# Row pitch of a resident matmul operand: 642 elements widened to 656

## The chip, the cores and the metric

The kernel runs on one core of a Trainium2 chip. The metric is the device time of one execution in microseconds (us). A "step" below is the time from the start of one matmul to the start of the next, read from the trace record by record, in nanoseconds (ns). Step lists and sums of steps are worked out from those records. They stand in ordinary fences, and lines copied from the profile in fences marked as such.

## The reference, cut to what matters

Input x is 2048 x 640, bf16. The result is `g * a + (1 - g) * b`, with a gate g, a linear attention a, and an MLP mixer b.

```python
qkv = (x @ wqkv)...                       # 32 heads of 20
pq, pk = phi(q), phi(k)
kv = einsum("bhsd,bhse->bhde", pk, v)     # the sum over s
z  = pk.sum(over s)
a  = (pq @ kv) / (pq @ z + 1e-6) @ wo
b  = x1 + gelu(layernorm(x1) @ w3) @ w4,  x1 = x + shifted(gelu(layernorm(x) @ w1)) @ w2
```

Since v = x @ wv, the sum over s can be taken first: `pk.T @ v = (pk.T @ x) @ wv`. The kernel does that. Its "g units" compute `pk.T @ x`, with a column of ones beside x that gives z for one more column in every second matmul (in the changed kernel the steps of 321 columns are 136.5 ns in the mean, those of 320 columns 136.0). A stretch of the kernel that does one such job is called a stage. The matmuls of the g units have x as their *moving operand* (`rhs` in the code), and `pk` as their weights (`lhsT`).

## The kernel before

x stays in SBUF for the whole kernel, as 16 chunks of 128 rows. Each partition holds one row of each chunk, one after the other. D is 640, and two elements follow each row: the first is the one for z.

```python
x_sb = const.tile([P, NCH, D + 2], BF16)           # P = 128, NCH = 16
...
nc.gpsimd.memset(x_sb[:, :, D:D + 1], 1.0)
...
def g_unit(j):                                      # five of them, HD = 320
    pt = pair()                                     # [P, 2, 512] f32 in PSUM; each half is called a bank
    for c in range(NCH):
        w = pk[:, c, :].rearrange("p (m j) -> p j m", j=DC)[:, j]    # every fifth column
        for hf in range(2):                         # left half, then right half with the ones
            nc.tensor.matmul(pt[:, hf, 0:HD + hf], lhsT=w,
                             rhs=x_sb[:, c, hf * HD:(hf + 1) * HD + hf],
                             start=(c == 0), stop=(c == NCH - 1))
    nc.scalar.copy(gs[...], pt[:, :, 0:HD]); ...    # then a DMA transpose into gT for the kv unit
```

## Time and profile before

| | before |
|---|---|
| time, median of 3 | 265.18 us (265.01 to 265.31) |
| span of the profiled run | 263.1 us |
| PE busy | 258.1 us, 98% |
| g stage (first g matmul to first w1 matmul) | 22.13 us |
| DVE, ACT busy | 54%, 31% |

These lines are from the profile page of the kernel before: engines' busy time, and the head of the chain that ended last.

```profile
PE 258.1 (98%) x1721; PEld 160.1 (61%) x1740; DVE 142.7 (54%) x282; ACT 82.7 (31%) x123; POOL 20.0 (8%) x65
...
PE 96%; DMA 2%; ACTq 1%; issue 1%; DVE 0%
```

TensorE does nearly all of the last chain (96%), so the time moves only with the length of matmuls or with a new wait. Next, the same chain in order of time, three of its pieces (start us, duration us, what):

```profile
2.25 4.14 DMA x_sb<-in_A_x_dram
...
7.00 20.72 PE pp L186 x152
...
49.30 22.13 PE pp L315 x160
```

L315 is the matmul of the g units: 160 of them in 22.13 us. (This view dates the piece at 49.30 us, some 0.16 us after the start of its first matmul in the records, 49.14 us.) The view of one source line gives their durations (ns min/median/max) and forms:

```profile
L315 PEld LDWEIGHTS <-pk x160: 117/117/120, 48.9 to 71.0; 128*128 128x128 bf16 x160
L315 PE MATMUL pp<-x_sb,pk x160: 297/300/302, 49.1 to 71.1; 128*128 128x320 bf16 x80, 128*128 128x321 bf16 x80
```

A matmul's 300 ns overlap with those of its neighbours, which start 135 to 140 ns apart. What counts is the step. These are the steps of one g unit of the kernel before, one pair (left, right) per chunk. The first line has the steps of chunks 0 to 3, the last the sums of all pairs:

```
c = 0..3     135 136   140 139   139 139   138 140
sums of pairs, c = 0..15:
271 279 278 278   271 279 279 279   271 278 278 278   272 280 277 278
```

Chunk c starts 1284c bytes into the tile, and the tile itself at a multiple of 64 (byte 16512 of a partition). So chunks 0, 4, 8 and 12 start on a multiple of 16 bytes. Those are the quick ones (271 or 272 ns a pair, against 277 to 280). A "16-byte line", or "line", below is a stretch of 16 bytes that begins on such a multiple.

### The profile page before, as it was taken

What the parts mean: (1) busy time and instruction counts of PE and PEld (TensorE: products, weight loads), DVE (VectorE), ACT (ScalarE), POOL (GpSimd) and SP (SyncE); (2) the same over time, 40 slices, a digit from 0 to 9 for tenths busy, and PEclk for the clock granted to TensorE, in tenths of its full rate; (3) what the DMA queues carried; (4) which work ended last, traced back from release to release, by engine and by line L of the source; (5) the groups of instructions that cost most, each with busy time, mean ns of one, the idle gap of its engine ahead of it and who ended that gap; (6) DMA issues with size and microseconds to landing.
All of it is one profiled execution on the core that took longest, in us unless ns stands there. A gap on an engine that the chain in (4) does not pass through costs nothing.

```text
span 263.1 us, 4250 instructions
## 1 busy us (share of the span) xinstructions
PE 258.1 (98%) x1721; PEld 160.1 (61%) x1740; DVE 142.7 (54%) x282; ACT 82.7 (31%) x123; POOL 20.0 (8%) x65
## 2 busy tenths in 40 slices
PE   8999999999999999999999999999999999999995
PEld 4777555688755644555577555577565577555553
DVE  1788778899947997955403464413356233112132
ACT  1555554321166236622502222412131332142200
POOL 5000230012210041001000001000001000000000
PEclk9999999999999999999999999999999999999999
DMA  7999995056672566700132000051100051100011
GB/s 210 214 196 363 379 283 218 0 27 125 125 98 57 104 124 148 257 0 2 25 75 77 25 0 2 0 100 52 50 0 2 1 100 52 50 0 2 0 50 50
DMA packets 45758, 23.98 MB, mean 91 GB/s; under 512 B 35115, under 2 KB 44971, under 8 KB 45739
## 3 DMA queue, kind: packets, MB, share of 16 engines
q1 hardware_dynamic: 45296, 23.22, 35.5%
q10 hardware_dynamic: 442, 0.49, 0.5%
q8 instruction: 13, 0.21, 0.4%
q14 instruction: 7, 0.05, 0.1%
HBM read 12.21 MB, written 2.62 MB: 56 GB/s over the span
## 4 chain that ended last, share of the span: by engine, by line
PE 96%; DMA 2%; ACTq 1%; issue 1%; DVE 0%
PE pp L500 22%; PE pp L467 21%; PE pp L315 8%; PE pp L451 8%; PE pp L420 8%; PE pp L349 8%; PE pp L243 8%; PE pp L186 8%; DMA x_sb<-in_A_x_dram 2%; PE pp L387 1%; PE pp L475 1%; PE pp L509 1%; PE pp L368 1%; PE pp L258 0%; ACTq L125 0%
## 5 line engine op out<-in xcount | busy, mean ns | idle before, releaser
L467 PE MATMUL pp<-lnxT,w_sb 128*128 128x512 bf16 x249 | 59.8, 379 | 0.6
L500 PE MATMUL pp<-w_sb,h 128*128 128x384 bf16 (+3 forms) x414 | 57.6, 299 | 0.2 <-issue 0.2
L469 ACT ACTIVATE h<-pp 128x1024 bf16<-128x1024 f32 (+1 forms) x28 | 26.9, 962 | 82.2 <-PE pp L467 82.2
L500 PEld LDWEIGHTS <-h 128*128 128x128 bf16 x416 | 38.3, 98 | 19.3 <-issue 1.1
L467 PEld LDWEIGHTS <-w_sb 128*128 128x128 bf16 x260 | 25.5, 98 | 26.8
L514 DVE SCALAR_TENSOR_TENSOR oc<-pp,omg,x 128x640 bf16<-128x640 f32 (+2 forms) x20 | 14.4, 748 | 45.1 <-ACT h2x L478 21.3
L454 DVE SCALAR_TENSOR_TENSOR x<-pp,gate,x 128x640 f32<-128x640 f32 x16 | 13.9, 867 | 29.4 <-PE pp L451 29.4
L178 ACT ACTIVATE e<-pp 128x640 bf16<-128x640 f32 (+1 forms) x26 | 21.5, 827 | 9.6 <-PE pp L243 9.6
L451 PE MATMUL pp<-m_sb,pqT 128*128 128x320 bf16 x160 | 24.3, 299 | 0.0
L420 PE MATMUL pp<-w_sb,hsT 128*128 128x320 bf16 x160 | 23.9, 299 | 0.0
L423 DVE TENSOR_TENSOR x<-pp,x_sb 128x640 f32<-128x640 f32 x16 | 13.1, 820 | 19.7 <-PE pp L420 19.7
L186 PE MATMUL pp<-wk_sb,xT 128*128 128x320 bf16 (+1 forms) x160 | 22.6, 299 | 0.1
L315 PE MATMUL pp<-x_sb,pk 128*128 128x320 bf16 (+1 forms) x160 | 22.3, 300 | 0.0
L243 PE MATMUL pp<-xT,hsT 128*128 128x512 bf16 x98 | 21.6, 379 | 0.1
L315 PEld LDWEIGHTS <-pk 128*128 128x128 bf16 x160 | 18.8, 117 | 3.5
L420 PEld LDWEIGHTS <-hsT 128*128 128x128 bf16 x160 | 15.7, 98 | 8.2
L451 PEld LDWEIGHTS <-pqT 128*128 128x128 bf16 x160 | 15.7, 98 | 7.7
L186 PEld LDWEIGHTS <-xT 128*128 128x128 bf16 x160 | 15.6, 98 | 6.6 <-DVE xT L219 0.4
L349 PE MATMUL pp<-lnxT,w_sb 128*128 128x512 bf16 x76 | 17.9, 379 | 0.2
L243 PEld LDWEIGHTS <-hsT 128*128 128x128 bf16 x100 | 11.8, 118 | 9.7
L285 POOL TENSOR_SCALAR rstd<-mv 128x4 f32<-128x4 f32 (+1 forms) x11 | 3.4, 313 | 155.5 <-DVE mv L291 155.5
L180 DVE SCALAR_TENSOR_TENSOR pk<-pp,e 128x640 bf16<-128x640 f32 x16 | 13.2, 823 | 1.7
(76 smaller groups left out, 190.3 us busy)
## 6 DMA issues: line engine op xcount, KB each, us to landing
out_dram<-oc SPq DMA_DIRECT2D x14, 160.0 KB, 1.8
w_sb<-in_B_w_dram SPq DMA_DIRECT2D x1, 2160.0 KB, 8.4
w_sb<-in_B_w_dram SPq DMA_DIRECT2D x1, 2080.0 KB, 10.4
x_sb<-in_A_x_dram SPq DMA_DIRECT2D x1, 1280.0 KB
x_sb<-in_A_x_dram SPq DMA_DIRECT2D x1, 960.0 KB, 7.1
wo_sb<-in_A_wo_dram SPq DMA_DIRECT2D x6, 160.0 KB, 7.6
hsT<-in_A_wqkv_dram SPq DMA_DIRECT2D x1, 800.0 KB, 5.7
m_sb<-in_A_wqkv_dram SPq DMA_DIRECT2D x1, 800.0 KB, 11.6
```

Of the source, the lines that this page charges most:

```text
L178: nc.scalar.activation(ev, src, ACT.Exp)
L186: nc.tensor.matmul(pt[:, hf, 0:n], lhsT=xT[:, dc, c * P:(c + 1) * P], rhs=wk_sb[:, dc, hf * HD:hf * HD + n], start=(dc == first), stop=(dc ...
L243: nc.tensor.matmul(pt[:, t % 2, :], lhsT=wq_sb[:, dc, :].rearrange("p (m j) -> p j m", j=DC)[:, j], rhs=xT[:, dc, t * TS:(t + 1) * TS], st ...
L315: nc.tensor.matmul(pt[:, hf, 0:HD + hf], lhsT=w, rhs=x_sb[:, c, hf * HD:(hf + 1) * HD + hf], start=(c == 0), stop=(c == NCH - 1))
L349: nc.tensor.matmul(pt[:, i, :], lhsT=w, rhs=lnxT[t][:, dc, :], start=(dc == 0), stop=(dc == DC - 1))
L420: nc.tensor.matmul(pt[:, hf, 0:HD], lhsT=hsT[:, fc, 2 + c * P:2 + (c + 1) * P], rhs=w2_sb[:, fc, hf * HD:(hf + 1) * HD], start=(fc == 0), ...
L451: nc.tensor.matmul(pt[:, hf, 0:HD], lhsT=pqT[:, j, c * P:(c + 1) * P], rhs=m_sb[:, j, hf * HD:(hf + 1) * HD], start=(j == 0), stop=(j == D ...
L454: nc.vector.scalar_tensor_tensor(x1, pt[:, :, 0:HD], gate[:, c:c + 1], x1, op0=ALU.mult, op1=ALU.add)
L467: nc.tensor.matmul(pt[:, k, :], lhsT=w3_sb[:, dc, fc * P:(fc + 1) * P], rhs=lnT[:, dc, :], start=(dc == 0), stop=(dc == DC - 1))
L469: nc.scalar.activation(h2[:, 2 * i * TS:(2 * i + n) * TS], pt[:].rearrange("p h e -> p (h e)")[:, 0:n * TS], ACT.Gelu_apprx_tanh)
L500: nc.tensor.matmul(dst, lhsT=st[t]["h2"][:, fc * TS + cc * P:fc * TS + (cc + 1) * P], rhs=w4_sb[:, fc, a:b], start=start and fc == 0, stop ...
L514: nc.vector.scalar_tensor_tensor(oc[:, a:b], src, omg[:, c:c + 1], st[t]["x1"][cc][:, a:b], op0=ALU.mult, op1=ALU.add)
```

## The change

The intent: start every row of x on an aligned address. 656 elements are 1312 bytes, a multiple of 16 and of 32.

```diff
-    x_sb = const.tile([P, NCH, D + 2], BF16)
+    x_sb = const.tile([P, NCH, D + 16], BF16)
```

Nothing else changes. All engines' instructions keep their order, and later tiles move by 448 bytes, a multiple of 64.

## The prediction

> **What bounds the kernel.** TensorE. The page has PE busy 258.1 us of a 263.1 us span (98%), its granted clock at nine tenths or more in every slice; VectorE has 54%, ScalarE 31%. The chain that ended last is 96% PE, and the list of waits gives PE's matmuls about 1 us of waiting in all, nearly all before 6.5 us. So time changes only if matmuls get shorter, or if something now in time becomes late.
>
> **What the change touches.** No instruction is added, removed or reordered (the order on every engine is the same). Chunk c of the resident x moves from byte 1284c to byte 1312c of a partition; later tiles move by 448 bytes, a multiple of 64. 1284c is a multiple of 16 only for c = 0, 4, 8, 12; 1312c always is. Readers of x: five g units (160 matmuls, x as moving operand), bn_stats and the layernorm's tensor_scalar, the residual add, ten small matmuls at the start.
>
> **TensorE.** The g units run from 49.14 to 71.27 us, back to back. The start-to-start times of their 160 matmuls (read record by record) have a strict period of four chunks: the two matmuls of chunks 0, 4, 8 and 12 take 135.5 and 136.5 ns, those of other chunks 138 to 140 (mean about 139.3). Chunk 4 starts on 16 bytes but not on 32, and is as fast as chunk 0, so 16 is the granule. [...] With the new pitch every chunk is on the granule: 120 matmuls save about 3.3 ns each, 0.40 us. The g stage should take 21.7 us, mean step 135.9 ns in place of 138.3.
>
> **Is it on the critical path?** After the g units PE goes straight on. The first thing that could be late is the kv unit (first weight load at 76.45 us), which needs the last transposed g: it lands at 75.74 us and hangs on VectorE and the DMA queue (the copy before it waited 4.8 us for a transfer), so it does not move with PE. Slack shrinks from 0.7 to about 0.3 us, still enough. Later PE waits for nothing. So the whole 0.4 us should reach the end.
>
> **The rest.** The layernorm's tensor_scalar takes 390 to 450 ns, bn_stats 440 to 490, and neither follows the period of four; I expect no change, and VectorE does not bound. The 1280-byte DMA packets take a median of 55 ns (60 when queues are full), x and weights alike: no gain seen. x of chunks 2 to 15 lands long before 49 us. Chunk 1's landing (6.4 us) gates TensorE briefly at the start; faster writes could give at most 0.2 us there. I count none.
>
> **Prediction.** 265.18 - 0.40 = 264.8 us, range 264.3 to 265.3. Chances: faster by over 2% 0.01, within 2% 0.98, slower by over 2% 0.01.
>
> **What would show it right or wrong.** Right: the g matmuls all step at 135 to 137 ns, without the period; the stage is 0.4 us shorter; the first w1 matmul and all after it are 0.4 us earlier; other groups keep their means. Wrong: the period stays (then it is not the start address but, say, the weights' read); the kv unit gets a wait of 0.4 us; the residual add (820 ns) or bn_stats gets shorter.
>
> **What would make the prediction wrong.** A spread between executions (0.3 us in the three times of before) as large as the effect; DMA landings at the start that shift by some tenths; a second granule at 32 or 64 bytes, which chunk 4 speaks against.

## More of the kernel before

The w2 stage (and the attention stage, which is built alike) has the halves as the outer loop. Its moving operand has a pitch of 640 elements:

```python
for hf in range(2):
    for fc in range(DC):                            # DC = 5
        nc.tensor.matmul(pt[:, hf, 0:HD], lhsT=hsT[:, fc, ...],
                         rhs=w2_sb[:, fc, hf * HD:(hf + 1) * HD], start=..., stop=...)
```

## The result, and the profile after

In the rounds of the prediction the changed kernel took 264.84 us in the median (264.66 to 265.43, 4 runs) and the kernel before 265.10 us (264.95 to 265.31, 4 runs). The ratio is 0.9993, with a 95% interval of 0.9976 to 1.0011. The median lies within 0.1 us of the prediction. Whether there is any gain at all, these eight times alone don't say. The trace does.

The page after, the same lines:

```profile
PE 257.7 (98%) x1721; PEld 160.1 (61%) x1740; DVE 142.7 (54%) x282; ACT 82.7 (31%) x123; POOL 20.0 (8%) x65
...
PE 96%; DMA 2%; ACTq 1%; issue 1%; DVE 0%
```

The chain in order of time, after:

```profile
2.25 4.48 DMA x_sb<-in_A_x_dram
...
7.34 20.72 PE pp L186 x152
...
49.65 21.80 PE pp L315 x160
```

And the g matmuls' durations after:

```profile
L315 PEld LDWEIGHTS <-pk x160: 117/117/120, 49.3 to 71.0; 128*128 128x128 bf16 x160
L315 PE MATMUL pp<-x_sb,pk x160: 299/300/301, 49.5 to 71.1; 128*128 128x320 bf16 x80, 128*128 128x321 bf16 x80
```

The g stage is 0.33 us shorter (21.80 against 22.13), and the median duration of its matmuls is the same 300 ns: the change shows only in the steps. But in this profile everything began 0.34 us later, because chunk 1 of x landed later (the DMA piece took 4.48 us, not 4.14), and the two spans are both 263.1 us. A reader who compares spans alone would call the change worthless. The steps of one unit after:

```
c = 0..3     136 137   136 136   136 137   136 136
```

The period is gone. Two things were left to settle: is the later start part of the change, and what exactly is paid for off the 16-byte line?

### The profile page after: what moved, and what is told of

Read it like the earlier page. It is cut to its first block, busy times and chain, and to the rows that moved or that the text cites. A ratio compares the mean times of both kernels' runs of the same rounds, so it can differ in the third digit from the quotient of the medians.

```text
span 263.1 us, 4250 instructions
## 1 busy us (share of the span) xinstructions
PE 257.7 (98%) x1721; PEld 160.1 (61%) x1740; DVE 142.7 (54%) x282; ACT 82.7 (31%) x123; POOL 20.0 (8%) x65
## 4 chain that ended last, share of the span: by engine, by line
PE 96%; DMA 2%; ACTq 1%; issue 1%; DVE 0%
PE pp L500 22%; PE pp L467 21%; PE pp L315 8%; PE pp L420 8%; PE pp L451 8%; PE pp L349 8%; PE pp L243 8%; PE pp L186 8%; DMA x_sb<-in_A_x_dram 2%; PE pp L387 1%; PE pp L475 1%; PE pp L509 1%; PE pp L368 1%; PE pp L258 0%; ACTq L125 0%
```

## The experiments

All runs are summed up here, from their traces. "Rest" is the time from the end of the g stage to the end of the last matmul. It is the same within 3 ns in all kernels that touch only the g stage, so all that the g stage saves or loses reaches the end.

| run | what | g stage, us | rest, us | g stage begins at, us |
|---|---|---|---|---|
| before | pitch 642 | 22.134 | 189.086 | 49.14 |
| after | pitch 656 | 21.800 | 189.087 | 49.48 |
| again | pitch 656 | 21.800 | 189.087 | 49.20 |
| p648 | pitch 648 | 21.800 | 189.087 | 49.48 |
| off4B | pitch 656, all 4 bytes off | 21.971 | 189.086 | 49.18 |
| w642 | 656; other operands at 642 | 21.800 | 189.135 | 49.43 |
| even322b | 642, 322 columns | 22.134 | 189.086 | 49.61 |
| contigwb | 642, contiguous weights | 22.105 | 189.085 | 49.37 |
| p644b | pitch 644 | 21.998 | 189.086 | 49.54 |
| off2Bb | pitch 656, all 2 bytes off | 22.104 | 189.084 | 50.59 |
| hfouter | 642, halves outside | 21.802 | 189.085 | 49.35 |
| both320 | 642, 320 + 320 columns | 22.016 | 189.084 | 49.58 |
| inner642 | as w642, halves inside | 21.800 | 189.512 | 49.87 |
| orders | 642, five orders | 21.888 | 189.085 | 49.18 |

My first theory was that of the prediction: a moving operand that starts off a 16-byte line costs some 3 ns per matmul. A first attempt at four of the runs got no chip. They were submitted again unchanged, with a b at the end of the label.

### again: the start-up

No edit.

> The changed kernel once more, to separate its effect from the start-up. Start-address theory: the g stage (first g matmul to first w1 matmul) takes 21.80 us as in the first profile of it, against 22.13 before; the start (first k matmul of the long run, 6.83 us before and 7.18 in the first profile after) is noise of the DMA landings, so it varies by some tenths and is not tied to the pitch. Time 0.2 to 0.4 us under before, about 264.8. Rival (the change itself delays chunk 1 of x by 0.35 us): the long k run starts at about 7.2 us again, and the time is equal to before within 0.1 us.

Measured: stage 21.800 us as before. It began at 49.20 us instead of 49.48, with the very same kernel. The chain of this run has these pieces:

```profile
2.25 4.20 DMA x_sb<-in_A_x_dram
...
7.06 20.72 PE pp L186 x152
...
49.36 21.80 PE pp L315 x160
```

Over all fourteen profiles the stage begins anywhere between 49.14 and 50.59 us, and kernels whose rows of x all start on 16 bytes stand at 49.20 to 49.87, the others at 49.14 to 50.59. In the profiles whose chain has the landing of x as a piece, it is 4.14 to 5.59 us long. So the later start of the first profile after is scatter of the first DMA landings, and no effect of the pitch is seen in it. Time: 264.81 us (264.51 to 265.23, 6 runs) against 265.30 (264.85 to 268.42, 11 runs) for the kernel before. The ratio is 0.9956, 0.9914 to 0.9998. Several runs of the kernel before were over 266 us in that session, so this ratio flatters the change. The lowest times, 264.51 against 264.85, differ by the 0.34 us that the stage shows, but the start-up scatters by as much, so that agreement proves nothing.

### p648: which granule

```diff
-    x_sb = const.tile([P, NCH, D + 16], BF16)
+    x_sb = const.tile([P, NCH, D + 8], BF16)
```

> Row pitch 648 elements (1296 bytes): every chunk starts on 16 bytes, every second one not on 32. Start address with a granule of 16 bytes: every g matmul steps at 136 to 137 ns, the stage takes 21.80 us, time as the changed kernel. Rival, granule 32 bytes: half of the chunks stay at about 139 ns, stage about 22.0 us. Rival, the shift of all later tiles by 448 bytes did it: here they shift by another amount (192), so nothing certain, but the stage would not follow the 16-byte rule.

Measured: stage 21.800 us, pairs of 272 and 273 ns in all chunks; 264.84 us (264.44 to 265.10). A pitch of 1296 bytes, a multiple of 16 but not of 32, was enough here: 1312 bytes, a multiple of both, gave the same 21.800 us.

### off4B: the pitch or the start

```diff
-    x_sb = const.tile([P, NCH, D + 16], BF16)
+    x_all = const.tile([P, NCH, D + 16], BF16)
+    x_sb = x_all[:, :, 2:D + 16]
```

> Pitch 656 kept, but x starts 2 elements (4 bytes) into each row: no chunk starts on 16 bytes though the pitch is a multiple of 32. Start-address theory: all 160 g matmuls step at 139 to 140 ns, stage about 22.3 us, 0.5 us more than the changed kernel and 0.15 to 0.2 more than before; time about 265.3. Rival (the pitch counts, as a stride between chunks): the stage stays at 21.80 us and all steps at 136 to 137 ns.

Measured: stage 21.971 us; 264.88 us (264.66 to 265.41). Neither theory. The start does count, as the stage is 0.17 us over the aligned one at the same pitch. But the cost is a third of the expected 0.5 us, and it is uneven: every left half takes 135 ns and every right half 139 to 140.

### w642: the reverse, at scale

```diff
-    w2_sb = const.tile([P, DC, D], BF16)
+    w2_sb = const.tile([P, DC, D + 2], BF16)
-    m_sb = const.tile([P, DC, D], BF16)
+    m_sb = const.tile([P, DC, D + 2], BF16)
-    w4_sb = w4p.tile([P, FF + 1, D], BF16)
+    w4_sb = w4p.tile([P, FF + 1, D + 2], BF16)
     ... their loads and the copy into m_sb write [..., 0:D]
```

> The reverse at scale: on the changed kernel, the moving operands of the w2, attention and w4 stages get the pitch of 642 elements. 96 + 96 + 320 = 512 matmuls then start off the 16-byte line. Start-address theory as a property of any moving operand: each takes about 2.9 to 3.3 ns more, whatever its width (256 to 512 columns), 1.5 to 1.7 us in all, time about 266.4; chunks 0, 4, 8, 12 of each keep 136 ns for 320 columns. If the penalty goes with the columns, the 512-column ones pay 1.6 times what the 320-column ones pay. Rival (it is special to the g stage, where weights are read with a stride of 10 bytes and their loads take 117 ns): no change, time about 264.8.

Measured: 264.79 us (264.34 to 265.18), a clear miss. 512 matmuls off the line cost 0.05 us in all, not 1.6. Here is one w2 unit (first line: left halves, second: right halves), and one run of 13 matmuls of the w4 stage (384 columns each; fc = 0 to 12):

```
w2    136 136 138 135 135
      135 136 138 135 135
w4    174 162 165 162 161 162 165 162 161 162 165 162 161
```

The first w4 step is the stage's entry. After it a period of four is visible, but one long step is made good by a short one: 162 + 165 + 162 + 161 = 650 ns, just as 163 + 162 + 163 + 162 in the aligned kernel. So the start off the line alone cost next to nothing here (0.05 us over 512 matmuls, 0.1 ns each). My theory had fallen. Something of the g stage had to be added to the misalignment, and four things were special there: odd widths, strided weights, the order of the halves, and widths that differ.

### even322b and contigwb: odd width, strided weights

```diff
even322b
-    nc.gpsimd.memset(x_sb[:, :, D:D + 1], 1.0)
+    nc.gpsimd.memset(x_sb[:, :, D:D + 2], 1.0)
-    ... pt[:, hf, 0:HD + hf], ... x_sb[:, c, hf * HD:(hf + 1) * HD + hf]
+    ... pt[:, hf, 0:HD + 2 * hf], ... x_sb[:, c, hf * HD:(hf + 1) * HD + 2 * hf]
contigwb
-    w = pk[:, c, :].rearrange("p (m j) -> p j m", j=DC)[:, j]
+    w = pk[:, c, j * P:(j + 1) * P]
```

> The kernel before, pitch 642 kept, with one edit: the second matmul of each g chunk takes 322 columns in place of 321 (the second spare column is set to one as well, and its sum is not read). What the earlier runs left: with x 4 bytes off the line in every chunk only the 321-column matmuls were slow (139.5 ns, the 320-column ones 135), and in the w2, attention and w4 stages misaligned even widths cost nothing on average. Theory A (an odd width off the line costs, even ones don't): the period of four goes, all steps at 135 to 137.5 ns, stage 21.8 to 21.9 us. Theory B (the strided weight loads of this stage, 117 ns in place of 98, collide with misaligned moving reads): the steps stay at 138 to 140 ns in three chunks of four, stage 22.1 us.

> The kernel before, pitch 642 and 321 columns kept, but the weights of the g stage are read as contiguous columns of pk in place of every fifth one. The result is wrong on purpose. Theory A (odd width): the period of four stays, stage about 22.1 us, though weight loads fall from 117 to 98 ns. Theory B (strided weight loads): the period goes, all steps at 136 to 137 ns, stage 21.8 us.

Measured: stage 22.134 us with 322 columns, exactly as before, and 22.105 with contiguous weights, whose loads did fall from 117 to 98 ns. Both keep the period (pairs of 271, 279, 278, 279 and 271, 278, 278, 277). Each run names the other theory as the one that holds, and both theories are thereby out: strided weights are worth 0.03 us at most. (contigwb was meant to give a wrong result; the argument uses its steps alone.)

### p644b and off2Bb: other offsets

```diff
p644b
-    x_sb = const.tile([P, NCH, D + 16], BF16)
+    x_sb = const.tile([P, NCH, D + 4], BF16)
off2Bb
-    x_sb = const.tile([P, NCH, D + 16], BF16)
+    x_all = const.tile([P, NCH, D + 16], BF16)
+    x_sb = x_all[:, :, 1:D + 16]
```

> Row pitch 644 elements (1288 bytes): chunks start on the 16-byte line or 8 bytes off it in turn. Simple start-address theory (each misaligned matmul pays about 2.9 ns): stage 22.03 us with a period of two chunks. If a change of the offset from one chunk to the next is what costs (chunks all 4 bytes off paid only 1.1 ns per matmul, those of before 2.1): nearly every chunk pays, stage 22.1 us or more.

> Pitch 656, x 1 element (2 bytes) into each row, so no access of x starts on 4 bytes. TensorE: as with 4 bytes off, 320 columns at 135 to 136 ns and 321 columns at 139 to 140, stage about 21.97 us. [...] DMA landings unchanged within some tenths of a us.

Measured: 21.998 us at pitch 644, period two (pairs of 271 and 279). That is what the simple theory said (22.03), and here only the chunks off the line pay. With x 2 bytes off everywhere the stage took 22.104 us (pairs of 276 ns, left 136 and right 140), 0.13 more than I expected. The run was also to show whether VectorE's operations on x get longer when no row starts on 4 bytes. They don't; the view of the x tile in this run has:

```profile
L290 DVE BATCH_NORM_STATS2 st1s<-x_all x16: 439/485/490, 53.5 to 72.4; 128x6 f32<-128x320 bf16 x16
...
L306 DVE TENSOR_SCALAR ln<-x_all,mv,rstd x16: 395/441/448, 59.1 to 89.5; 128x640 bf16<-128x640 bf16 x16
```

The same view of the kernel before:

```profile
L289 DVE BATCH_NORM_STATS2 st1s<-x_sb x16: 440/485/489, 52.1 to 71.0; 128x6 f32<-128x320 bf16 x16
...
L305 DVE TENSOR_SCALAR ln<-x_sb,mv,rstd x16: 394/442/448, 57.6 to 88.1; 128x640 bf16<-128x640 bf16 x16
```

The medians are 441 and 442 ns for the layernorm's operation. This one execution took 266.19 us because its g stage began 1.4 us late; x and the weights of the k stage landed late (x chunk 1 5.6 us after its issue, 4.1 in the kernel before; the weights' three loads on the SP queue a median of 5.0 us, 3.7 before), and with one look I can't say whether the 2-byte starts had a part in it. (GpSimd's memset of the ones also waited here, 27.3 us for x, and ran at 28.7 us, still long before the g stage.)

### hfouter, both320 and inner642: the order of the halves

```diff
hfouter (on the kernel before)
-        for c in range(NCH):
-            w = ...
-            for hf in range(2):
+        for hf in range(2):
+            for c in range(NCH):
+                w = ...
both320 (on the kernel before)
-    ... pt[:, hf, 0:HD + hf], ... x_sb[:, c, hf * HD:(hf + 1) * HD + hf]
+    ... pt[:, hf, 0:HD], ... x_sb[:, c, hf * HD:(hf + 1) * HD]
-    ... hmask[:], pt[:, 1, HD:HD + 1])
+    ... hmask[:], pt[:, 1, HD - 1:HD])
inner642 (on w642; w2 stage, and the attention stage alike)
-        for hf in range(2):
-            for fc in range(DC):
+        for fc in range(DC):
+            for hf in range(2):
```

> The kernel before, pitch 642 and widths kept, but in each g unit the two half rows are the outer loop: first all 16 chunks of the left half, then all 16 of the right, as the w2 stage orders its own. Both earlier ideas fell (with 322 columns, and with contiguous weights, the period of four stayed). Theory C (what exposes the misaligned start is the order: two half rows back to back, which alternates the PSUM bank and lets the second matmul begin in the 16-byte line where the first ended): the steps off the line fall to within about 1 ns of those on it, the stage to 21.8 to 21.9 us. Theory D (the unequal widths, 320 and then 321 or 322 columns): the left-half run of 16 is free of it, the right-half run keeps steps of 139 to 140 ns in three of four, stage about 22.0 us.

> The kernel before, pitch 642 and order kept, but both half rows take 320 columns: the column of ones is left out and the sums are read from the last x column in its place, so the result is wrong on purpose. Theory C (order): steps stay at 138 to 140 ns in three chunks of four; stage about 22.1 us. Theory D (unequal widths): the period goes, steps about 136 ns, stage about 21.75 us.

> The kernel of run w642 (w2, attention and w4 operands at pitch 642, x at 656), with the half rows made the inner loop in the w2 and attention stages, as the g stage has it; all widths are 320 there. In w642 the mean step of these stages was 135.98 ns, 0.14 ns over the aligned 135.84. Theory C (order): the 192 matmuls off the line now take about 139 ns, so the mean step of both stages rises to about 137.5 ns and the time grows by about 0.5 us. Theory D (unequal widths): the mean stays at 136.

Measured: with the halves outside, at the old pitch of 642 with 120 matmuls off the line, the stage took 21.802 us. That is the whole gain of the change without the change. The chain of hfouter:

```profile
7.21 20.72 PE pp L186 x152
...
49.52 21.80 PE pp L315 x160
```

With equal widths (both320; relative error 17.6, wrong) the period stayed, and the stage took 22.016 us. At 135.84 ns a step, the mean of the 320-column matmuls of the w2 stage in the changed kernel, it would be about 21.73 us (an estimate from that step). And with the halves inside, the w2 and attention stages began to pay: mean step 137.35 and 137.33 ns against 135.98 and 135.99 in w642, rest 189.512 us. The first four w2 units in the chain, kernel w642:

```profile
87.64 5.43 PE pp L420 x40
```

and kernel inner642:

```profile
88.08 5.48 PE pp L420 x40
```

5.43 became 5.48 us for 40 matmuls. (This view shows little of it; the sums of steps show 0.38 us over the rest of the kernel.) hfouter and inner642 thus agree that it is the order that makes a start off the line cost, and both320 that unequal widths are not needed for it.

### orders: what about the order

That order differs in more than one way: the PSUM bank alternates, the same weights are loaded twice, each offset comes twice, and the right half begins in the 16-byte line in which the left one ended. This run gives each g unit its own order, at pitch 642.

```diff
-        for c in range(NCH):
-            w = ...
-            for hf in range(2):
+        order = ([(c, hf) for c in cs for hf in (0, 1)],
+                 [(c, hf) for c in cs for hf in (1, 0)],
+                 [(c if hf == 0 else (c + 8) % NCH, hf) for c in cs for hf in (0, 1)],
+                 [(c, hf) for hf in (0, 1) for c in twice],         # 0, 4, 1, 5, 2, 6, 3, 7, 8, 12, ...
+                 [(c + i, hf) for c in range(0, NCH, 2) for hf in (0, 1) for i in (0, 1)])[j]
+        for c, hf in order:
+            w = ...
     ... (cut: cs = range(NCH), the list twice, and start and stop by each half's own first and last)
```

> Pitch 642, all widths and the result as before, but each of the five g units runs its 32 matmuls in another order. Unit 0: as before (control), 278 to 279 ns per pair off the line, unit about 4.43 us. Unit 1: the halves swapped within a chunk (right, then left), so that the second does not begin in the line where the first ended. Unit 2: left half of chunk c, then right half of chunk c+8: bank alternates at every matmul, but the weights differ and no line is shared; the offset from the 16-byte line is the same in both. Unit 3: left halves first, then right, but chunks in the order 0, 4, 1, 5, 2, 6, 3, 7 and so on, so that each offset comes twice in a row, with one bank for 16 matmuls. Unit 4: two left, two right, so the bank changes at every second matmul, and the offsets go 0, 4, 0, 4, 8, 12, 8, 12 bytes. Shared line: only units 1 to 3 (not 0 and 4... 4 shares none either) are free of the penalty: unit 0 4.43, the others about 4.36 us. The same weights twice: units 0 and 1 pay (4.43), units 2, 3, 4 don't. Bank alternation: units 0, 1 and 2 pay (4.43), 3 does not (4.36), 4 pays about half or none. Sequence of offsets (each twice): units 0, 1, 2 and 3 pay, 4 need not.

Measured, from the records:

```
unit  order                                         us
0     left c, right c (as before)                   4.427
1     right c, left c                               4.362
2     left c, right c+8                             4.360
3     all left, then all right, offsets in twos     4.366
4     two left, two right                           4.373
(aligned kernel, every unit                         4.360)
```

Unit 0 alone pays in full. Unit 1 differs from it in nothing but which half comes first: the bank still alternates, the weights still repeat, the offsets still come in twos. So bank, weights and offsets are out. What is left is the 16-byte line: in unit 0 a matmul starts in the line in which the one before it ended. The result is correct. The kernel took 264.57 us.

The records say more than that the right half pays for following its left half. At pitch 642 a row's right half ends 2 bytes before the next row, so the left half of the next chunk too starts in the line in which the matmul before it ended, unless its row starts on a line, and it pays as well (138.9 ns in the kernel before). Sorting the matmuls off the line by this, with addresses worked out from the pitch, the widths and the order, gives these mean steps (ns):

```
                     starts in a new line     starts in the line where the last one ended
before               -                        left 138.9, right 139.6
p644b                -                        left 139.7, right 139.4
off4B                left 135.0               right 139.6
off2Bb               left 135.9               right 140.4
both320              left 135.5 (1, 5, 9, 13) left 138.8, right 139.2
inner642, w2 + att.  left 135.9 (fc, j = 1)   left 138.4, right 139.1
hfouter              left 136.1, right 136.9  -
```

The aligned kernel has 136.0 and 136.5. (even322b and contigwb sort as before does, within 0.4 ns.) The row of both320 is the sharpest. Its right halves are one column shorter, so that of chunk 0 ends exactly at a line's end. The left half of chunk 1 starts at byte 1284, as in the kernel before. It takes 135.5 ns here (mean of chunks 1, 5, 9 and 13), and took 139.7 there, where the column of ones reaches into its line. A piece that merely adjoins the last one doesn't pay either: in the changed kernel each right half adjoins its left half, but on a line's edge, and takes 136.5 ns.

The expectation of this run held that unit 4 shares no line. That was an error: the left halves of chunks 2, 6, 10 and 14 follow there on the right halves of chunks 1, 5, 9 and 13. Four such starts fit its 13 ns over the aligned unit, though other single steps of that unit reach 138 to 139 ns as well.

## Why the prediction was right

- **Bound by TensorE, no new wait: right.** Rest is 189.086 us before and 189.087 after. In both runs of the changed kernel the kv unit, where I feared a wait, starts its matmuls 5.40 us after the g stage, as before (76.67 less 71.27, 5.39 by the records).
- **Period and granule: right.** The period of four is gone after the change, 648 elements do as well as 656, and 644 gives a period of two.
- **Size: 0.33 us instead of 0.40.** The mis-sized term is "120 matmuls save about 3.3 ns each". A pair off the line went from about 278.5 to 272.5 ns, so 3.0 ns each. Also, a pair on the line took 271 ns among pairs off it and takes 272.5 among its like, so the 40 aligned matmuls gave back about 0.7 ns each. Per unit that is 12 x 6.0 - 4 x 1.5 = 66 ns (4.427 less 4.360 us measured: 67). I had taken the steps of the aligned chunks in the mixed trace for those that a fully aligned one would have.
- **Mechanism: half right.** "The start address costs" held in these runs only where the matmul before ended in the same 16-byte line (mean steps of 138.4 to 140.4 ns, against 135.0 to 136.9 elsewhere, by the table under orders). The prediction's reading, a penalty on each matmul off the line, would have given 1.6 us in w642, where 0.05 us was measured. The trace before could not have told: all its 120 matmuls off the line are also such starts. That the price per matmul could be read there and carried over to the change was luck in this respect.
- **VectorE and DMA: right in that no effect is seen.** The layernorm's operation stays at 439 to 442 ns; the start of the g stage scatters with either pitch (49.14 to 50.59 us). The 0.2 us that the prediction names for faster writes was its estimate; in the waits of the kernel before, PE's matmul at L214 waits 0.2 us for x.

What stays open: why a start in the line in which the matmul before ended costs anything. That it does fits all the runs of the table under orders, but no run looks into the reads themselves. It also accounts for a riddle: with a constant offset only the right half of each pair pays (2.1 ns per pair at 4 bytes in off4B, 3.8 at 2 bytes in off2Bb), while at pitch 642 and 644 both halves do (5.6 and 5.0 ns per pair off the line; each worked out from the stage over that of the aligned kernel). Why 2 bytes cost more than 4 is unexplained, and so are the 6 ns that unit 3 of orders keeps.

No version beats the changed kernel clearly: hfouter at the old pitch and 656 or 648 elements in the old order all reach 21.80 us.

## What to carry to other kernels

In these runs matmuls were some 3 ns longer where their moving operand started in the 16-byte line in which that of the matmul before ended. If a trace of yours shows such steps, try a pitch and pieces that begin on 16 bytes (21.800 us here), or an order in which neighbours don't follow each other (21.802 us): each removed the whole cost here, 0.33 us of 22.134. It was small, about 2% of the steps concerned (278.5 ns a pair against 272.5). When an effect is smaller than the scatter of the start-up, compare the length of the stage between two fixed events in the trace and show that the rest is equal; spans can hide it. And when a periodic cost matches an address pattern, put the same pattern into another stage before you call it a cost of the address: here that run was the one which refuted the simple reading.
